# A fused attention and gated feed-forward kernel: the test of the limits moves from ahead of the banded path to behind it, and the planner gets a new table of ranks

## The chip, the cores and the metric

The kernel runs on one core of one Trainium2 chip. The metric is the device time of one execution in microseconds (us); lower is better. TensorE is called PE below (PEld is its weight load), VectorE DVE, ScalarE ACT, GpSimd POOL and SyncE SP.

## The reference

Attention with a few sink columns and a window, then a feed-forward layer. All inputs are float32 except the feed-forward weights, which are float64, and the two limits, which are 64-bit integers.

```
B, H, S, D = 4, 8, 768, 64          # n_sink = 4, window = 128
scores = q @ k.T / sqrt(D)
keep   = (col < n_sink) | ((0 <= row - col) & (row - col < window))
a      = softmax(where(keep, scores, -1e9))
x      = (a @ v) as (B*S, H*D) = (3072, 512)
h      = x @ w_in                   # (512, 2048)
g      = h * tanh(softplus(h))
y      = g @ w_out                  # (2048, 512)
```

## The kernel before

There are two paths in the program. `Fast` is the banded path: it is right when `n_sink <= 8`, `1 <= window <= 128`. `General` computes any limits. Both stand in the program as straight code without loops.

`body` starts with the prologue. SP issues the load of the limits (L978), then the keys, queries and values of the first two pairs of heads (L989 to L992). ACT loads its table (L981), writes two elements into each of three weight buffers (L985) and issues three loads of weights into them (L987, tiles `raw`). PE runs `WARM` = 24 products of zeros (L1000, "warm-ups") ahead of the first work. DVE builds constants, turns the limits into floats (L1004), makes a flag out of them in three small steps (L1009 to L1011) and then the three masks m0, m1, m2 (L961 to L968). Then each of the five engines reads the flag into a register (L1013), compares and branches (L1014): `Fast` follows straight on, `General` stands behind it and is jumped over at the end of `Fast`.

`Fast` cuts the work into 12 chunks of 256 rows, and in each chunk into four pairs of heads. For a pair, PE makes the scores (L442 for the first chunk of a batch, L445 for the others), DVE adds the mask and takes the row's minimum (L459), ACT the exponential (L462), DVE the reciprocal of the sum (L467, L468), DVE or ACT the normalisation (L476, L477), PE transposes (L487), ACT or DVE copies the result (L292, L294, L295) and PE multiplies by the values (L521). Next to that the weights, which come as float64, are taken apart into a high and a low part by ACT, DVE and POOL (L327 to L348, and the helpers L292, L295, L303, L305). The feed-forward layer runs per chunk in steps: L570 (first product), the activation in ACT and DVE (L580 to L587), L609 (second product). The last chunks end with L659 and L678, the scaling at L668 and the stores of y at L634 and L671.

The order of all this is not written by hand. Every operation is a task with a rank, the engines that may do it and a time; `Plan.solve` places the tasks one after the other, always the one that could start first, with `TILT` times its rank added. The ranks come from the tables `WI`, `WO` (weights) and `PAIRS` (pairs of heads), `EARLY` and `RING` hold when the loads of the prologue are expected, and `BANKS` says which PSUM buffers some tiles use. Where the plan leaves PE idle for more than `SPARE` = 250 ns, `emit` puts in products of zeros (L771, "fillers"), 75 of them in this kernel. Each engine then runs its tasks strictly in the plan's order.

## Time and profile before

| | |
|---|---|
| median of 3 runs | 690.08 us (689.73 to 690.75) |
| the profiled execution | 690.23 us, of which the profile's span is 688.4 us |
| PE busy | 679.2 us (99% of the span) |
| ACT busy | 525.4 us (76%) |
| DVE busy | 501.8 us (73%) |
| POOL busy | 124.4 us (18%) |

Shares are means over a front in which PE waits for the others and a long rest in which it does not, so they are to be read by stretch. The 1.8 us between the span and the execution's own time lie outside of what the profiler shows. A "PE busy" counts fillers and warm-ups too.

### The profile page before, as it was taken

Reading aid. Unit: us, or ns where it says so; the run is one execution under the profiler, and the core shown is the slowest. Engines: PE = TensorE matmul, PEld = TensorE weight load, DVE = VectorE, ACT = ScalarE, POOL = GpSimd, SP = SyncE. Lnnn points to the kernel's source line nnn. Section 1 sums busy time; section 2 is a strip of 40 time slices with the busy share of each in tenths; the row PEclk is TensorE's granted clock in tenths of the full one; section 3 lists DMA queues with packets and bytes.
Section 4 is the critical chain, followed back from the end, with each engine's and each line's share of the span. In section 5 each row is a group of like instructions: output and inputs, shape, how many; then the busy total and the mean of one; then the engine's idle time right before and its main releaser. Section 6 shows DMA issues by size and latency. Waiting matters only on the chain.

```text
span 688.4 us, 12130 instructions
## 1 busy us (share of the span) xinstructions
PE 679.2 (99%) x3980; PEld 563.6 (82%) x3980; DVE 501.8 (73%) x1442; ACT 525.4 (76%) x1223; POOL 124.4 (18%) x128
## 2 busy tenths in 40 slices
PE   8999999999999999999999999999999999999997
PEld 6778888988888888887888888887888787888885
DVE  8999999999896887666875886667677567432342
ACT  6999898987977876767876886778777676666672
POOL 1422321121104233120132131222010110000000
PEclk9999999999999999999999999999999999999999
DMA  6564343343535334041323331133340300010001
GB/s 211 175 185 124 123 139 114 116 135 98 161 97 156 88 83 134 16 110 39 95 79 91 112 86 55 40 86 95 101 109 1 86 0 25 1 62 0 1 0 67
DMA packets 49272, 60.20 MB, mean 87 GB/s; under 512 B 4912, under 2 KB 42160, under 8 KB 49200
## 3 DMA queue, kind: packets, MB, share of 16 engines
q1 hardware_dynamic: 48624, 57.69, 29.2%
q10 hardware_dynamic: 576, 1.64, 0.6%
q8 instruction: 34, 0.56, 0.3%
q14 instruction: 38, 0.31, 0.1%
HBM read 53.02 MB, written 6.29 MB: 86 GB/s over the span
## 4 chain that ended last, share of the span: by engine, by line
PE 84%; ACT 9%; DVE 5%; DMA 1%; issue 1%; ACTq 0%
PE hp L570 31%; PE acc L609 22%; PE att L609 12%; PE att L521 5%; PE att L445 5%; PE att L570 3%; ACT p L462 3%; PE att L487 2%; ACT p L477 1%; PE att L525 1%; ACT w L292 1%; ACT pth L292 1%; DMA raw<-w_in 1%; DVE u L587 1%; PE busy L1000 1%; ACT u L582 1%
## 5 line engine op out<-in xcount | busy, mean ns | idle before, releaser
L570 PE MATMUL hp<-w,w 128*128 128x256 f32 (+1 forms) x1440 | 269.8, 335 | 0.0
L570 PEld LDWEIGHTS hp<-w,w 128*128 128x128 f32 x1440 | 220.2, 189 | 28.3 <-issue 1.0
L609 PE MATMUL acc<-w,gh 128*128 128x512 f32 x500 | 137.9, 400 | 0.8 <-ACT w L292 0.5
L609 PEld LDWEIGHTS acc<-w,gh 128*128 128x128 f32 x500 | 87.7, 188 | 19.3 <-ACT gh L292 1.6
L462 ACT ACTIVATE p<-p,nm 128x136 f32<-128x136 f32 (+2 forms) x192 | 80.4, 428 | 21.2 <-DVE nm L459 20.6
L582 ACT ACTIVATE u<-u,bias 128x512 f32<-128x512 f32 x96 | 69.5, 724 | 35.0 <-DVE u L581 34.8
L587 DVE SCALAR_TENSOR_TENSOR u<-u,hp 128x512 f32<-128x512 f32 x88 | 60.1, 683 | 40.4 <-ACT u L586 37.8
L292 ACT ACTIVATE gh<-u 128x512 fp32r<-128x512 f32 x88 | 55.8, 634 | 33.7 <-DVE u L587 31.5
L580 ACT ACTIVATE u<-hp 128x512 f32<-128x512 f32 x88 | 52.5, 596 | 33.6 <-PE hp L570 32.0
L609 PE MATMUL acc<-w,gl 128*128 128x512 f32 x250 | 75.5, 394 | 0.0
L305 DVE TENSOR_TENSOR gl<-u,gh 128x512 fp32r<-128x512 f32 x72 | 51.8, 720 | 29.8 <-PE att L609 14.5
L584 ACT ACTIVATE u<-u,bias 128x512 f32<-128x512 f32 x96 | 69.6, 725 | 2.1
L303 POOL TENSOR_TENSOR w<-raw,w 64x400 fp32r<-64x400 f32 (+1 forms) x40 | 45.6, 1145 | 135.4 <-ACT w L292 50.9
L581 DVE TENSOR_SCALAR u<-u 128x512 f32<-128x512 f32 x96 | 43.0, 448 | 34.1 <-ACT u L580 33.7
L609 PE MATMUL att<-w,gh 128*128 128x512 f32 x244 | 67.5, 394 | 0.0
L586 ACT ACTIVATE u<-u 128x512 f32<-128x512 f32 x96 | 60.7, 632 | 1.9
L459 DVE CUSTOM_DVE_ANT_0 p<-att,m 128x136 f32<-128x136 f32 (+2 forms) x192 | 54.9, 313 | 3.1 <-PE att L442 1.2
L609 PEld LDWEIGHTS acc<-w,gl 128*128 128x128 f32 x250 | 46.2, 188 | 9.1 <-DVE gl L305 0.2
L457 DVE COPY_PREDICATED att<-behind,att 128x128 f32<-128x128 int32 x128 | 34.4, 292 | 25.6 <-PE att L445 25.0
L609 PEld LDWEIGHTS att<-w,gh 128*128 128x128 f32 x244 | 44.6, 188 | 8.8
L445 PEld LDWEIGHTS att<-w,w 128*128 128x128 f32 x256 | 41.1, 188 | 7.4 <-PE att L609 0.4
L445 PE MATMUL att<-w,w 128*128 128x264 f32 x256 | 45.8, 287 | 0.0
(115 smaller groups left out, 958.3 us busy)
## 6 DMA issues: line engine op xcount, KB each, us to landing
raw<-k_p SPq DMA_DIRECT2D x64, 200.0 KB, 3.4
raw<-q_p SPq DMA_DIRECT2D x64, 128.0 KB, 3.1
raw<-w_out SPq DMA_DIRECT2D x15, 512.0 KB, 3.6
raw<-w_in SPq DMA_DIRECT2D x14, 512.0 KB, 3.5
vt<-v_b SPq DMA_DIRECT2D x32, 192.0 KB, 2.6
y<-u SPq DMA_DIRECT2D x20, 256.0 KB, 2.1
ks<-k_p SPq DMA_DIRECT2D x16, 132.0 KB, 2.8
qh<-q_p SPq DMA_DIRECT2D x16, 128.0 KB, 2.9
```

Of the source, the lines that this page charges most:

```text
L292: ways[ACT] = act_t(n, psum), lambda: nc.scalar.activation(dst(), src(), AF.Copy, scale=scale or 1.0)
L305: way = dve_t(n), lambda: nc.vector.tensor_tensor(dst(), a(), b(), ALU.subtract)
L445: yield nc.tensor.matmul(st[e].t, part.t[:, e, cols], ks[e].t[:, c0:c0 + n], start=n_ == 0, stop=n_ == 1)
L459: a = add(r(.03 + .01 * e), {DVE: (dve_t(nw) + 8, lambda st=st, pv=pv, nm=nm, e=e, mask=mask, n=n, nw=nw: nc.vector.tensor_tensor_reduce(o ...
L462: a = add(r(.05 + .01 * e), {ACT: (act_t(nw, ptr=2), lambda pv=pv, nm=nm, i=i, e=e: nc.scalar.activation(pv(), pv(), AF.Exp, bias=nm.t[:, ...
L570: yield nc.tensor.matmul(out, w_.t[:, fs], x_, start=kt == 0 and n_ == 0, stop=kt == KT - 1 and n_ == 2)
L580: a = add(r + .5, {ACT: (act_t(N, True), lambda: nc.scalar.activation(u.t, hp.t, AF.Exp))}, g1, [hp], [u])
L582: sq = add(r + .52, {ACT: (act_t(N, ptr=1), lambda: nc.scalar.activation(u.t, u.t, AF.Square, bias=self.one)), DVE: shared((dve_t(N), lamb ...
L584: a = add(r + .53, {ACT: (act_t(N, ptr=1), lambda: nc.scalar.activation(u.t, u.t, AF.Ln, bias=self.half if sq.eng == ACT else self.one, sc ...
L586: a = add(r + .54, {ACT: (act_t(N), lambda: nc.scalar.activation(u.t, u.t, AF.Exp, scale=-1.0))}, [a], [u])
L587: e = add(r + .55, {DVE: (dve_t(N), lambda: nc.vector.scalar_tensor_tensor(u.t, u.t, 1.0, hp.t, ALU.subtract, ALU.mult))}, [a], [u, hp])
L609: yield nc.tensor.matmul(acc[at].t, g_.t[:, y, ts_], w_.t, start=new and n_ == 0, stop=done)
```

## The change

The flag and the branch go from ahead of `Fast` to behind it. `Fast` follows the prologue without a branch. Its last DVE operation is followed by the three steps that make the flag, then every engine reads it, compares, and jumps over `General` when the banded path was right (`General` would write y once more). The load of the limits moves from SP's queue to ACT's, ahead of ACT's table load. The part of the masks that only later chunks need (m2) becomes a task of the plan (`far`). `WARM` goes from 24 to 16. The planner gets new numbers (ranks, `EARLY`, `RING`, `BANKS`, two penalties), start times for ACT and DVE (`START`), and counts PE's tasks double for the first 1.5 us (`COLD`).

```diff
-WI = -8.52, -5.11, -2.45, -0.51, 7.12, ...
+WI = -13.89, -6.84, 0.25, -0.85, 5.69, ...
-PAIRS = (-17.41, -16.23, -9.53, ...
+PAIRS = (-15.84, -15.34, -4.82, ...
-WARM, SPARE, ROOM = 24, 250, 7
+WARM, SPARE, ROOM = 16, 250, 9
+START, COLD, FAR = {ACT: 550, DVE: 600}, 1500, 2
...
-        free = {e: 0.0 for e in (PE, ACT, DVE, POOL, SP)}
+        free = {e: START.get(e, 0.0) for e in (PE, ACT, DVE, POOL, SP)}
...
-            dur = t.ways[e][0]
+            dur = t.ways[e][0] * (2 if e == PE and at < COLD else 1)
...
+        self.plan.add(FAR, {DVE: shared((300, lambda: c.far()))})
...
+    def far():
         drop(c.m2[:, SK:], near, window)
-        behind(nc.vector.tensor_copy(c.m2[:, 0:SK], col[:, 0:SK]))
+        nc.vector.tensor_copy(c.m2[:, 0:SK], col[:, 0:SK])
...
-        nc.sync.dma_start(raw, limits.bitcast(I32).partition_broadcast(P))
+        nc.scalar.dma_start(raw, limits.bitcast(I32).partition_broadcast(P))
...
-            ok = tmp.tile([P, 1], F32, name="ok")
...
-            ready = nc.vector.scalar_tensor_tensor(flag, window_f, float(P), ok, ALU.is_le, ALU.mult)
-            c.masks(lambda x: tc.add_manual_dep(x.ins, ready.ins.name, nosync, reason="plan"))
-        banded = nc.values_load(flag[0:1, 0:1], min_val=0, max_val=1)
-        with tc.If(banded > 0) as cmp:
-            with ExitStack() as c2:
-                Fast(c2, tc, q, k, v, vs, w_in, w_out, out, c).run()
-        with cmp.Else():
+            c.masks()
+        with ExitStack() as c2:
+            Fast(c2, tc, q, k, v, vs, w_in, w_out, out, c).run()
+        ok, flag = top.tile([P, 1], F32, name="ok"), top.tile([P, 1], I32, name="flag")
+        nsink_f, window_f = lim[:, 0:1], lim[:, 1:2]
+        last = c.last[nc.vector.engine]
+        for ins in (nc.vector.tensor_scalar(ok, nsink_f, float(SK), None, ALU.is_le),
+                    nc.vector.scalar_tensor_tensor(ok, window_f, 1.0, ok, ALU.is_ge, ALU.mult),
+                    nc.vector.scalar_tensor_tensor(flag, window_f, float(P), ok, ALU.is_le, ALU.mult)):
+            tc.add_manual_dep(ins.ins, last.name, nosync, reason="plan")
+            last = ins.ins
+        banded = nc.values_load(flag[0:1, 0:1], min_val=0, max_val=1)
+        with tc.If(banded < 1):
             with ExitStack() as c2:
                 General(c2, tc, q, k, v, vs, w_in, w_out, out, c).run()
```

From the diff's first function on, line numbers of the changed kernel are 1 to 7 higher (L442 is L444 there, L459 L461, L668 L670).

The first place is the start of ACT's program, from its table load to its first normalisations. `raw_66` to `raw_68` are the three weight buffers, `p_...` the scores of a pair of heads (the first two pairs follow each other), `nm` their row minima. Before:

```order
L981 ACT_TABLE_LOAD
...
L987 DMA raw_68<-w_in 128x1024
L1013 TENSOR_LOAD flag
L1014 COMPARE_AND_BRANCH
L462 ACTIVATE p_11_0_196,sm_1_197<-p_11_0_196,nm_2_198 128x128 x2
L462 ACTIVATE p_11_0_196,sm_1_197<-p_11_0_196,nm_0_213 128x256 x2
L462 ACTIVATE p_22_0_217,sm_1_218<-p_22_0_217,nm_2_219 128x128 x2
L327 ACTIVATE w_0_237<-raw_67 128x512
```

And now:

```order
L984 DMA lim_raw<-limits 128x4
L987 ACT_TABLE_LOAD
...
L993 DMA raw_68<-w_in 128x1024
L464 ACTIVATE p_11_0_164,sm_1_165<-p_11_0_164,nm_2_166 128x128 x2
L329 ACTIVATE w_0_186<-raw_66 128x512
L464 ACTIVATE p_17_0_182,sm_1_183<-p_17_0_182,nm_2_184 128x128 x2
L464 ACTIVATE p_11_0_164,sm_1_165<-p_11_0_164,nm_0_194 128x256 x2
```

The flag's read and branch are gone from here, the limits' load stands first, and ACT's third operation of the path is now a step on the first weight buffer, `raw_66`, which DVE did before (L328).

The second place is PE's program from its last warm-up on; `att_...` are scores, `ks_60`, `qh_62` the first pair's keys and queries, `ks_61`, `qh_63` the second's. Before:

```order
L1000 MATMUL busy<-zero 128x224
L1013 TENSOR_LOAD flag
L1014 COMPARE_AND_BRANCH
L442 MATMUL att_0_188<-ks_60,qh_62 128x128
L442 MATMUL att_1_189<-ks_60,qh_62 128x128
L442 MATMUL att_0_192<-ks_60,qh_62 128x256
L442 MATMUL att_1_193<-ks_60,qh_62 128x256
...
L442 MATMUL att_0_206<-ks_61,qh_63 128x128
```

And now:

```order
L1005 MATMUL busy<-zero 128x224
L444 MATMUL att_0_158<-ks_60,qh_62 128x128
L444 MATMUL att_1_159<-ks_60,qh_62 128x128
...
L444 MATMUL att_0_170<-ks_61,qh_63 128x128
L444 MATMUL att_1_171<-ks_61,qh_63 128x128
L444 MATMUL att_0_178<-ks_60,qh_62 128x256
L444 MATMUL att_1_179<-ks_60,qh_62 128x256
```

The second pair's narrow scores now stand ahead of the first pair's wide ones. Over the whole path PE's program holds 75 fillers before and 69 now. Up to PE's first run of over fifty operations without a filler it is 60 before and 67 now; behind that run 15 before (4, and 11 ahead of one group of transposes) and 2 now.

The third place is the end of the path: DVE's last operations and what SP does behind its last store (`y`). On DVE before, and then now:

```order
L668 SCALAR_TENSOR_TENSOR w_0_7932<-att_0_7919,w_0_7873 128x128
L668 SCALAR_TENSOR_TENSOR w_0_7934<-att_0_7919,w_0_7873 128x128
L1014 UNCONDITIONAL_BRANCH
```

```order
L670 SCALAR_TENSOR_TENSOR w_0_7900<-att_0_7885,w_0_7834 128x128
L1018 TENSOR_SCALAR ok<-lim 128x1
L1019 SCALAR_TENSOR_TENSOR ok<-lim,ok 128x1
L1020 SCALAR_TENSOR_TENSOR flag<-lim,ok 128x1
L1023 TENSOR_LOAD flag
L1024 COMPARE_AND_BRANCH
```

On SP, now:

```order
L673 DMA y<-w_0_7898 128x128
L1023 TENSOR_LOAD flag
L1023 ISA x2
L1024 COMPARE_AND_BRANCH
```

Before, SP's last store was followed by the unconditional branch alone; now the read of the flag, two register steps and the comparison stand between them.

## Rows read from the trace of the kernel before

**Rows 1.** Busy time by stretch: length, then each engine's busy us (instructions), PEclk, DMA
```profile
10.00:60.00 50.00, 48.30 (x378) 36.77 (x379) 47.78 (x181) 49.96 (x160) 16.80 (x13) 1.00 0.59 172
...
100.00:150.00 50.00, 49.42 (x313) 43.44 (x313) 48.75 (x101) 45.59 (x92) 9.81 (x8) 1.00 0.41 128
...
200.00:683.00 483.00, 482.76 (x2643) 398.41 (x2642) 315.63 (x921) 346.76 (x785) 78.22 (x85) 1.00 0.23 64
```

**Rows 2.** The chain of waits in the first 60 us, start us, us, what
```profile
7.11 1.93 ACT p L462 x8
...
41.78 1.22 PE att L771 x11
```

**Rows 3.** Timeline of the first 14 us: start us, us, engine, line, operation [idle before]
```profile
0.73 1.28 ACT L981 ACT_TABLE_LOAD   x1 [0.73 <-PEq L1024]
0.74 0.39 SPq L978 DMA_DIRECT2D lim_raw<-limits  x1
...
2.26 0.38 ACTq L987 DMA_DIRECT2D raw<-w_in  x1
...
2.60 0.44 SPq L990 DMA_DIRECT2D qh<-q_p  x1
...
3.46 0.16 DVE L1004 SCALAR_TENSOR_TENSOR lim<-lim_raw 128x2 f32<-128x2 int32 x1 [0.28 <-DMA lim_raw<-limits]
...
3.65 0.15 DVE L1009 TENSOR_SCALAR ok<-lim 128x1 f32<-128x1 f32 x1
...
4.11 0.28 DVE L961 TENSOR_SCALAR col<-col,lim 128x128 f32<-128x128 f32 x1
...
5.30 0.16 DVE L968 COPY m<-col 128x8 f32<-128x8 f32 x1
...
5.80 1.53 PE L442 MATMUL att<-ks,qh 64*128 64x128 f32 x8
6.71 0.29 DVE L459 CUSTOM_DVE_ANT_0 p<-att,m 128x128 f32<-128x128 f32 x1 [1.25 <-PE att L442]
...
7.11 0.40 ACT L462 ACTIVATE p<-p,nm 128x128 f32<-128x128 f32 x1 [4.69 <-DVE nm L459]
...
7.14 0.42 DVE L328 TENSOR_SCALAR w<-raw 128x512 f32<-128x512 f32 x1
...
11.38 2.18 PE L771 MATMUL acc<-zero 128*128 128x224 bf16 x21
```

**Rows 4.** The warm-ups by line: duration ns min/median/max, first and last start us
```profile
L1000 PE MATMUL busy<-zero x24: 366/394/394, 1.0 to 5.3; 128*128 128x224 bf16 x24
```

**Rows 5.** The page's DMA issues: count, KB each, median us to landing
```profile
qh<-q_p SPq DMA_DIRECT2D x16, 128.0 KB, 2.9
```

**Rows 6.** Loads of the weight buffers that start in the first 30 us, issue to landing
```profile
DMA to landing us min/median/max: 3.4/4.2/6.3
```

**Rows 7.** The last operations of the path, timeline from 676 us
```profile
683.38 0.49 DVE L668 SCALAR_TENSOR_TENSOR w<-att,w 128x128 f32<-128x128 f32 x2 [0.58 <-PE att L659]
683.91 0.37 ACTq L671 DMA_DIRECT2D y<-w  x1
```

**Rows 8.** Flag read, branch and closing block by line: ns min/median/max, first and last start
```profile
L1013 SPq TENSOR_LOAD <-flag x1: 468/468/468, 4.2 to 4.2; - x1
...
L1014 ACTq COMPARE_BRANCH  x2: 38/38/39, 5.0 to 684.3; - x2
L1014 SPq COMPARE_BRANCH  x2: 46/48/49, 5.1 to 684.3; - x2
...
L1053 SPq EVENT_SEMAPHORE  x18: 17/17/28, 5.2 to 688.4; - x18
...
L1053 ACTq DRAIN  x2: 8/38/67, 687.0 to 687.9; - x2
```

**Rows 9.** DVE groups by shape: busy us, mean ns of one, idle before
```profile
L476 DVE TENSOR_SCALAR p<-p,rc 128x136 f32<-128x136 f32 x67 | 16.7, 290 | 0.6
...
L305 DVE TENSOR_TENSOR vss<-qh,vss 64x128 fp32r<-64x128 f32 x14 | 3.7, 288 | 0.4 <-ACT vss L292 0.2
```

## The prediction

> **What bounds the kernel now.** I read busy time by stretch first. From 200 us to 683 us PE is busy for 482.76 of 483.00 us, so there nothing but PE's own work counts, and the change takes none of that away. From 10 to 60 us it is the other way: ACT is busy for 49.96 of 50.00 us and DVE for 47.78, while PE's 48.30 are partly fillers [rows 1]. The reader is to see two regimes: a front in which ACT is the bound and PE waits, and a rest in which PE is. In the second one an earlier start is kept and nothing more is won. Then the chain of waits: up to 60 us it runs mostly through ACT's exponentials, and at 41.78 us through 11 fillers, 1.22 us, which is PE waiting for a group of transposes [rows 2]. Last the two ends. In front the first row minimum on DVE starts at 6.71 us after 1.25 us of idle time, and ACT's first exponential at 7.11 us, after 4.69 us of waiting [rows 3]. At the end the path's last DVE operations run from 683.38 to 683.87 us, the last store is issued at 683.91 us, ACT and SP branch at 684.3 us, and the closing block ends at 688.4 us [rows 7, 8].

> **The front: an earlier start.** The three steps of the flag lie between 3.65 us, where the first starts, and 4.11 us, where the first mask does: 0.46 us. Without them the last mask, which starts at 5.30 us and takes 0.16, ends at 5.00 us. PE's warm-ups follow each other in (5.3 - 1.0) / 23 = 0.187 us [rows 4]; 16 of them end at about 4.0 us, where 24 kept PE until the first scores at 5.80 us. The first queries are loaded on SP's queue, which loses the limits' load of 0.39 us from its front, and their load takes 2.9 us [rows 5]; they are there at about 4.1 us. So the scores are done before the masks are, DVE can take the first minimum at 5.00 us instead of 6.71, and ACT the first exponential at 5.40 us instead of 7.11 [rows 3]: **1.71 us earlier**. The limits themselves are as early as before: they were first on SP's queue at 0.74 us and are first on ACT's now, and DVE waited 0.28 us for them.

> **What is late next.** ACT's queue now has the limits' load of 0.39 us ahead of the table load (1.28 us, which started at 0.73) and of all that follows, so the first weights are issued at 2.26 + 0.39 = 2.65 us. On SP that load held back the first queries; on ACT it holds back the weights. The new order puts a step on those weights third on ACT, behind two exponentials of 0.40 us, at 6.20 us. A weight load takes 4.2 us in the median, 3.4 at least [rows 6], and DVE read this buffer at 7.14 us without waiting, so it took at most 7.14 - 2.26 = 4.88 us. That gives a wait on ACT of 2.65 + 4.2 - 6.20 = **0.65 us**, between nothing and 1.33. What is queued behind it is the second pair's exponentials, and the chain of the front goes through them. I take the median: of the lead 1.71 - 0.65 = **1.06 us** is left (0.38 to 1.71). The second pair's narrow scores also move ahead of the first pair's wide ones on PE; its queries were issued at 2.60 us and by 2.9 us of loading are there at some 5.2 us, before ACT is free, so I give that no price.

> **The new order.** What it does to PE's waiting I price by the fillers, which stand where the plan leaves PE without work: 13 fewer behind the first long run, 7 more ahead of it. One takes 2.18 / 21 = 0.104 us [rows 3]. That is 1.35 us less waiting at one place and 0.73 more at the other, net **0.62 us** less. The bounds are 1.35 us won, if the 7 only stand in place of warm-ups, and 0.73 lost, if the wait of the 11 comes back elsewhere because ACT has no time to spare. I take the net, since it counts both. m2's two steps, now a task of the plan, still stand on DVE ahead of the first minimum, so they are in the 5.00 us above. Penalties, `BANKS` and the ranks past 100 us I cost at nothing: PE's own backlog covers them (482.76 of 483.00 us), and if that cover fails it is the second rival below.

> **The end: a later branch.** The flag's steps took from 3.65 us to the read's start at 4.2 us, 0.55 us. Behind an end of 683.87 us the flag is there at 684.4 us. SP began the read at 4.2 us and branched at 5.1 us: 0.9 us for the read (0.468), the two register steps and the comparison [rows 8]. So SP branches at 685.3 us instead of 684.3: **1.0 us** later. From a branch over `General` to the next row ACT needs 687.0 - 684.3 = 2.7 us; that jump was there before and stays, and the stores land behind it. Nothing else waits for the branch, but nothing hides it either: the closing block begins with it. The lower bound is 0.6 us (flag and read alone); the upper is 2.3 us, if five engines that jump at the same time need half of 2.7 us more. The closing waits on SP are 17 to 28 ns each and may come twice, eight of them, 0.2 us, inside that bound.

> [...] The rows say 0.9 us from read to branch [rows 8]. [...]

> **The sum.** Of the profiled execution: 690.23 - 1.06 - 0.62 + 1.0 = 689.55 us. That execution lies 0.15 us above the median of the runs, 690.08, so against the median it is **689.4 us**, a gain of 0.68 us or 0.1%. A measurement of this kernel can tell 0.2%, that is 1.38 us, from no change; this one lies inside.

> **The rivals.**

> *The front is worth all of it.* The first weights land in time, the whole 1.71 us reach PE, and the wait at 41.78 us is gone without return. For it: those 11 fillers are one piece of the chain [rows 2]. Against it: ACT's 49.96 of 50.00 us, which leave no room to do the same work sooner. 690.08 - 1.71 - 1.35 + 1.0 = 688.0 us.

> *DVE becomes the bound between 100 and 150 us.* By a count of both programs, DVE takes 13 more normalisations from ACT (88 before) and 12 more of the small subtractions from POOL (14 before). At 0.290 and 0.288 us [rows 9] these are 7.2 us more. Between 100 and 150 us DVE is busy for 48.75 of 50.00 us and PE idles for 0.58 [rows 1]; what falls there beyond 1.25 us PE has to wait for. It decides against the change from 0.68 + 1.38 = 2.06 us of such waiting, that is with 3.3 of the 7.2 us in this stretch; with 4.8 of them it is 690.08 - 0.68 + 3.55 = 692.95, some 693.0 us. Against it: DVE has 483.00 - 315.63 = 167.37 us of idle time behind 200 us, and most of the path's pairs lie outside the stretch.

> *PE stays slow in front.* The warm-ups go at 0.187 us for 224 columns, the pace of 1.2 GHz; the filler at 11.38 us takes 0.104, that of 2.4 GHz (granted clock 1.00 from 10 us on) [rows 1, 3, 4]. With 16 warm-ups, 3 fillers and a wait for the second pair's queries PE does less before the first transposes. If it stays at the lower pace over eight more scores like those at 5.80 us (1.53 us), up to 1.53 us of chain are added; I take 1.0, since ACT works on meanwhile. 690.08 - 0.68 + 1.0 = 690.4 us. [...]

> **How the numbers follow.** The forecast 0.47, the full front 0.27, the slow PE 0.15, the DVE bound 0.11. Faster by over 0.2% is the second case, slower the fourth, and the first and third are both within 0.2%: 0.27, 0.62, 0.11. The known bounds reach from 690.08 - 1.71 - 1.35 + 0.6 = 687.6 us to the fourth case. I leave 2 in 10 out, the outermost part of the full front and the DVE case, and give **687.9 to 690.9 us**.

> **What would show it.** Right: DVE's first minimum near 5.0 us and ACT's first exponential near 5.4; a gap on ACT behind two exponentials that the load of the first weights ends; no chain of 11 fillers near 40 us; reads of the flag behind 684 us less the lead, and from the last L670 to the end of the span 1.0 us more than the 5.0 us between 683.38 and 688.4. Wrong: a first exponential later than 6 us (queries or limits late), an end longer by more than 1.6 us, or waits of PE for DVE's rows between 100 and 150 us. What would upset the number most is the new order's work between 10 and 60 us, where I price only fillers and not what ACT has to do before PE's backlog is formed.

## The result, and the profile after

| | before | after |
|---|---|---|
| median of the runs | 690.28 us (689.73 to 690.75, 4 runs) | 699.25 us (698.14 to 700.24, 4 runs) |
| ratio | | 1.0130 (95% interval 1.0110 to 1.0149) |
| the profiled execution, its span | 690.23 us, 688.4 | 700.24 us, 698.4 |
| TensorE's last matmul of the path starts | 683.1 us | 687.8 us |
| from its end to the span's end | 5.1 us | 10.3 us |

The change made the kernel 1.3% slower. The forecast was 689.4 us with a range of 687.9 to 690.9. Of the 10.0 us between the two profiled executions 4.8 are there before TensorE (PE) ends its last matmul, and 5.2 come behind it. The profiled execution of the changed kernel is the slowest of its four runs, 1.0 us above their median.

**The front.** The first group is of the timeline of the first 13 us of the changed kernel (start us, us, engine, line, operation, idle time before and what ended it); it answers to [rows 3].

```profile
0.74 0.41 ACTq L984 DMA_DIRECT2D lim_raw<-limits  x1
...
2.71 0.34 ACTq L993 DMA_DIRECT2D raw<-w_in  x1
...
3.88 0.16 DVE L1009 SCALAR_TENSOR_TENSOR lim<-lim_raw 128x2 f32<-128x2 int32 x1 [0.70 <-DMA lim_raw<-limits]
...
5.26 1.78 PE L444 MATMUL att<-ks,qh 64*128 64x128 f32 x12
5.34 0.29 DVE L461 CUSTOM_DVE_ANT_0 p<-att,m 128x128 f32<-128x128 f32 x1
...
5.74 0.40 ACT L464 ACTIVATE p<-p,nm 128x128 f32<-128x128 f32 x1 [2.87 <-DVE nm L461]
...
6.98 1.80 PE L773 MATMUL acc<-zero 128*128 128x224 bf16 x17
...
8.06 0.68 ACT L329 ACTIVATE w<-raw 128x512 f32<-128x512 f32 x1 [1.45 <-DMA raw<-w_in]
...
8.78 0.43 DVE L332 TENSOR_SCALAR w<-w 128x512 int32<-128x512 int32 x1 [1.57 <-ACT w L329]
...
12.42 1.51 PE L489 MATMUL att<-ident,p 128*128 128x128 f32 x6 [3.64 <-ACT p L479]
```

The start is earlier as forecast: the first exponential at 5.74 us instead of 7.11. But two exponentials later ACT stands for 1.45 us until the first weights land: issued at 2.71 us, they are there at 8.06, 5.35 us later. The second pair's exponentials are queued behind that step, DVE waits for it too, and PE, whose 17 fillers end at 8.78 us, stands for 3.64 us. Its first transposes start at 12.42 us; in the kernel before, at 10.57 (PE's row of its timeline):

```profile
10.57 0.96 PE L487 MATMUL att<-ident,p 128*128 128x128 f32 x6 [0.70 <-DVE p L476]
```

What that does to PE's clock is in the busy times by stretch of the changed kernel (length, then PE, PE's weight loads, DVE, ACT and POOL busy, granted clock, DMA share, GB/s; the last two answer to [rows 1]).

```profile
5.00:10.00 5.00, 3.78 (x32) 2.88 (x30) 3.30 (x21) 2.82 (x12) 0.00 (x0) 1.00 1.00 350
10.00:15.00 5.00, 2.58 (x13) 2.37 (x14) 4.58 (x15) 4.83 (x14) 0.00 (x0) 0.65 0.63 191
15.00:20.00 5.00, 5.00 (x27) 3.29 (x27) 3.64 (x15) 4.30 (x14) 0.00 (x0) 0.50 0.06 23
20.00:25.00 5.00, 5.00 (x42) 4.09 (x39) 3.74 (x15) 3.78 (x13) 1.28 (x1) 0.83 0.57 157
100.00:150.00 50.00, 50.00 (x325) 45.31 (x324) 49.01 (x99) 43.29 (x77) 9.11 (x7) 1.00 0.41 126
200.00:688.00 488.00, 487.00 (x2666) 401.50 (x2664) 319.14 (x948) 353.60 (x805) 64.92 (x67) 1.00 0.23 64
```

The granted clock is 1.00 between 5 and 10 us and then 0.65, 0.50 and 0.83: (0.35 + 0.50 + 0.17) x 5 / 0.5 = 10.2 us at the lower level (0.50), from 11.5 us, where PE still stands, to 21.7 us. Between 15 and 20 us PE is busy all the time and ACT, with 4.30 of 5.00 us, is not: the two have changed places. Between 100 and 150 us PE is busy for 50.00 of 50.00 us, so the waits for DVE that one rival put there did not come. From 200 us on PE idles for 1.00 us, where it had idled for 0.24.

**The end.** These rows of the changed kernel give flag read, branch and closing block by line (ns min/median/max, first and last start); they answer to [rows 7, 8]. SP's closing block of the kernel before follows them.

```profile
L661 PE MATMUL att<-w,w x18: 277/283/283, 685.8 to 687.8; 128*128 128x256 f32 x18
...
L1023 SPq TENSOR_LOAD <-flag x1: 517/517/517, 689.1 to 689.1; - x1
...
L1024 SPq COMPARE_BRANCH  x1: 50/50/50, 690.0 to 690.0; - x1
L1024 SPq EVENT_SEMAPHORE  x8: 17/17/17, 693.8 to 694.3; - x8
...
L1060 SPq EVENT_SEMAPHORE  x2: 28/28/28, 694.4 to 694.5; - x2
...
L1060 SPq EVENT_SEMAPHORE  x8: 17/28/28, 697.1 to 698.3; - x8
```

```profile
L1053 SPq EVENT_SEMAPHORE  x10: 17/28/28, 687.1 to 688.4; - x10
```

SP branches 1.9 us behind PE's last matmul (0.9 before), its next instruction comes 3.8 us later (2.8 before), eight waits, which the kernel before has in its front (from 5.2 us on), take 0.6 us here, and two waits into the closing block SP stands for 2.6 us (the hole, below). 1.0 + 1.0 + 0.6 + 2.6 = 5.2 us. The stores are not what it stands for: the last has landed by 690.3 us. The transfers in two windows of the same trace, 690.3 to 692 us and 694 to 696 us (queue, kind, packets, MB, share), are those of instructions, on q14 in pieces of 8 KB (over the whole run 40 with 0.33 MB):

```profile
q14 instruction: 4, 0.03, 6.4%
q8 instruction: 1, 0.02, 4.4%
...
q14 instruction: 4, 0.03, 5.3%
q8 instruction: 1, 0.02, 4.5%
```

One batch starts 0.6 us behind SP's branch, at 690.6 us, another at 694.1 us, 0.4 us after SP has gone on; between 692.1 and 694.1 us there is none. That SP stands until such a batch can be used is my reading of these times; e5 tests it for the hole.

### The profile page after: what moved, and what is told of

Same layout as the page of the kernel before. It is cut to its first block, busy times and chain, and to the rows that moved or that the text cites. A ratio compares the mean times of both kernels' runs of the same rounds, so it can differ in the third digit from the quotient of the medians.

```text
span 698.4 us, 12093 instructions
## 1 busy us (share of the span) xinstructions
PE 680.4 (97%) x3966; PEld 564.1 (81%) x3966; DVE 507.2 (73%) x1463; ACT 528.4 (76%) x1221; POOL 109.2 (16%) x109
## 4 chain that ended last, share of the span: by engine, by line
PE 68%; ACT 2%; DVE 1%; POOL 0%; issue 0%; ACTq 0%; POOLq 0%
PE hp L572 25%; PE acc L611 15%; PE att L611 12%; PE att L447 4%; PE att L523 4%; PE att L572 3%; PE att L489 2%; PE att L527 1%; PE acc L680 1%; PE att L506 1%; ACT p L464 0%; PE att L661 0%; PE att L680 0%; DVE w L307 0%; ACT w L294 0%
## 5 line engine op out<-in xcount | busy, mean ns | idle before, releaser
L611 PE MATMUL acc<-w,gh 128*128 128x512 f32 x500 | 135.2, 396 | 0.0
L305 POOL TENSOR_TENSOR w<-raw,w 64x400 fp32r<-64x400 f32 (+1 forms) x34 | 38.0, 1122 | 174.9 <-ACT w L294 82.1
L461 DVE CUSTOM_DVE_ANT_0 p<-att,m 128x136 f32<-128x136 f32 (+2 forms) x192 | 55.1, 314 | 4.2 <-PE att L444 2.5
L305 POOL TENSOR_TENSOR gl<-u,gh 128x512 fp32r<-128x512 f32 x19 | 24.6, 1293 | 175.4 <-PE att L611 104.9
L459 DVE COPY_PREDICATED att<-behind,att 128x128 f32<-128x128 int32 x128 | 34.2, 292 | 18.8 <-PE att L447 18.2
```

Source lines behind the costliest of these rows:

```text
L305: ways[POOL] = pool_t(n), lambda: nc.gpsimd.tensor_tensor(dst(), a(), b(), ALU.subtract)
L461: a = add(r(.03 + .01 * e), {DVE: (dve_t(nw) + 8, lambda st=st, pv=pv, nm=nm, e=e, mask=mask, n=n, nw=nw: nc.vector.tensor_tensor_reduce(o ...
L611: yield nc.tensor.matmul(acc[at].t, g_.t[:, y, ts_], w_.t, start=new and n_ == 0, stop=done)
```

## The experiments

**Theory A**, stated ahead of the first runs: two costs with nothing to do with each other, the branch behind the path (5.2 us) and the late first weights with the clock that falls behind PE's stall (4.8 us). The rivals are named in the expectations. Medians below are of 4 runs unless said otherwise; the kernel before, timed beside them, had medians of 689.7 to 690.3 us.

**Parts of the change undone (e1 to e4).** e1 puts the test ahead again, e2 takes the tables, limits' queue and warm-ups of before, e3 is the changed kernel with one line back, e4 has no test:

```diff
-        nc.scalar.dma_start(raw, limits.bitcast(I32).partition_broadcast(P))
+        nc.sync.dma_start(raw, limits.bitcast(I32).partition_broadcast(P))
```

> The changed kernel's tables, order and limits' queue, with the test put back ahead of the banded path. Theory A (two separate costs: 5.2 us at the end from the branch behind the path, 4.8 us in front because the first weights come later than the order counts on, so that TensorE stands still and its clock falls to half for 10 us): the end's 5.2 us go, the front's stay, since the weights land when they did, near 8.0 us: 695 us (694 to 696), half clock still in the records from about 11.5 us. Rival B (the earlier start itself makes the front slow, because loads that now start before 7 us get in the way of the first weights): with the test ahead the loads start late again and both costs go: 690 to 691 us. Rival C (the new order is no worse and all of the loss is the branch): 689 to 690 us.

Measured: 694.58 us, ratio 1.0057 (1.0041 to 1.0074). Within theory A's range by the sum, but not by the parts: 7.1 us follow PE's last matmul, because here too SP stands in the closing block (1.8 us), and the front loses 2.2 us and not 4.8. PE's first scores start at 5.66 us instead of 4.26, the transposes at 12.53, PE stands for 2.54 us, and the granted clock is 1.00 in every stretch up to 680 us. Rival B's reason does not hold: the weights are taken at 8.17 us here and at 8.06 in the changed kernel, late in both. What goes with the earlier start is a stall that is 1.1 us longer, and the fall of the clock with it.

> The tables, limits' queue and 24 warm-ups of the kernel before, with the test behind the path. Theory A: the end costs its 5.2 us; in front the order of before meets an earlier start, wins up to 1 us if its first weights hold no one up and loses some if they do: 694 to 697 us, at full clock from about 7 us on. Rival B (the earlier start makes the front slow): 698 to 700 us, with half clock in the front. Rival C (the branch is all of the loss): 699 to 700 us.

Measured: 694.48 us, 1.0055 (1.0034 to 1.0075), with a granted clock of 1.00 in every stretch up to 680 us and 10.7 us behind PE's last matmul. The test's move alone costs 4.3 us in the tables of before. PE's last matmul starts at 681.6 us, 1.5 sooner than before, but that is hardly the move: PE's work is 0.3 us ahead up to 100 us, and the rest comes between 100 and 132 us, where PE is busy for 32.00 of 32.00 us here and in e8 and for 31.42 in the kernel before, which waits there for 0.5 us until ACT has done a step on a late weight.

> The changed kernel with the limits' load issued first on SP's queue again; nothing else changes. Theory A: the first weights' load is issued 0.4 us sooner and lands some 0.4 us sooner, the stall of TensorE shortens by as much, the clock still falls: 698.0 to 699.3 us, 0 to 1 us less than the changed kernel. Rival D (the limits' load ahead of the weights on ScalarE's queue is what makes them late): weights land near 6.5 us as before and most of the front's 4.8 us goes: 695 to 696 us.

Measured: 697.15 us, 1.0098 (1.0079 to 1.0116): 2.1 us less than the changed kernel, between theory A and rival D. ACT takes the weights 1.8 us sooner and without waiting:

```profile
6.27 0.65 ACT L329 ACTIVATE w<-raw 128x512 f32<-128x512 f32 x1
```

The wait that is left is PE's for the second pair's queries, 1.43 us up to 6.78 us, and the clock falls behind it too, for 3.4 us.

```diff
...
-        banded = nc.values_load(flag[0:1, 0:1], min_val=0, max_val=1)
-        with tc.If(banded < 1):
-            with ExitStack() as c2:
-                General(c2, tc, q, k, v, vs, w_in, w_out, out, c).run()
```

> The changed kernel without the three flag steps, the read, the branch and the general path: limits that ask for the general path are not served. It measures what the end costs in all. Theory A: the front is untouched and the end is that of a program with no branch: 5 us or more less than the changed kernel, 693 to 694.5 us. Recorded forecast (the later branch costs 1.0 us): 698 us. If the jump of 2.7 us that the kernel before has in its front falls on nothing either way, the end after TensorE's last matmul is about 5 us, as before.

Measured: 691.45 us (10 runs), 1.0018 (1.0007 to 1.0029), 1.6 us below theory A's range. Behind PE's last matmul are 3.4 us: at the end a branch behind the path costs 6.9 us, one ahead of it, with its jump over `General`, 1.7 (2.0 in e8, 2.4 in e7). PE's work ends 2.0 us sooner than in the changed kernel's profile. With it goes the clock, which is at half for 3.4 us only, though PE stalls nearly as long (3.32 us, transposes at 12.47); that the clock is the reason is inferred here and tested in e6.

**The hole in the closing waits (e5).** Dead instructions in SP's program, in the path that is not run:

```diff
         with tc.If(banded < 1):
+            for _ in range(14):
+                nc.sync.dma_start(raw, limits.bitcast(I32).partition_broadcast(P))
```

> The changed kernel with 14 more loads of the limits on SP's queue inside the general path, which is not run here: dead instructions that only push the closing block of SP's program further along. Theory A (the end pays for fetching instructions twice: once at the jump's target, and once more 10 instructions behind it, because a fetched piece of SP's program happens to end there): the jump's 3.7 us stay, the second hole of 2.7 us in SP's closing waits goes or moves: 696.5 us (696 to 697.2), and SP's closing waits then stand without a hole. Rival E (the hole is a wait for a semaphore of another engine or of a store): it stays between the same two waits, 699.3 us.

Measured: 695.70 us, 1.0081 (1.0056 to 1.0105); from PE's last matmul to the end 7.5 us, 2.7 less. SP's closing block of this kernel, by line as above:

```profile
L1024 SPq EVENT_SEMAPHORE  x8: 17/17/17, 692.5 to 693.0; - x8
...
L1062 SPq EVENT_SEMAPHORE  x10: 17/28/28, 693.1 to 694.3; - x10
```

Eighteen waits follow each other without a hole. Nothing that is executed was changed, so the hole is a matter of where the instructions lie, and rival E falls. That a piece of 8 KB ends there is theory A's reading, which the run fits. The other runs agree: of those with the branch behind the path, the four with dead loads (e5, e12, f4, g1) have no hole and the nine without have one of 1.3 to 3.2 us. (Of the 3.55 us that the median fell, 0.8 are not the hole; the profile shows half clock for 6.8 us where the changed kernel's had 10.2.)

**The clock (e6).** 30 more fillers in the changed kernel's first long run of them (`more` starts at 30):

```diff
-                    for _ in range(int((t.start - at - SPARE) / (n / (1.2 if at < SLOW else 2.4) + 2.5) + 1)):
+                    m = int((t.start - at - SPARE) / (n / (1.2 if at < SLOW else 2.4) + 2.5) + 1)
+                    if m > 9 and more:
+                        m, more = m + more, 0
+                    for _ in range(m):
```

> The changed kernel with 30 more filler matmuls on TensorE in its idle stretch ahead of the first transposes, about 3.1 us at the pace of 0.104 us; the weights land as late as before. Theory A (part of the front's loss is the clock that falls after TensorE has stood still): no half clock behind 11 us, the first transposes still near 12.4 us, 1.5 to 2.5 us less than the changed kernel: 697.3 us (696.7 to 698). Rival F (the stretch at half clock costs nothing, because ScalarE and VectorE set the pace there): 699.3 us, however the clock stands.

Measured: 697.19 us, 1.0102 (1.0076 to 1.0127), 2.06 us less than the changed kernel; the two sets of four runs overlap by 0.2 us. All of it lies ahead of the end: PE's last matmul starts 2.1 us sooner, and 10.4 us follow it. Busy times by stretch and the timeline's row of the first transposes:

```profile
10.00:15.00 5.00, 4.73 (x45) 4.13 (x44) 4.56 (x17) 5.00 (x17) 0.00 (x0) 1.00 0.54 185
15.00:20.00 5.00, 5.00 (x46) 3.62 (x45) 5.00 (x20) 5.00 (x17) 0.73 (x1) 1.00 0.32 92
```

```profile
12.64 0.97 PE L489 MATMUL att<-ident,p 128*128 128x128 f32 x6 [0.27 <-ACT p L479]
```

The transposes start no sooner, but the clock stays at 1.00 and six of them take 0.97 us instead of 1.51. Work that computes nothing made the kernel 2 us faster; rival F falls.

**The limits' load (e7, e9, f1).** e7 is the kernel before with that one load on ScalarE's queue.

> The kernel before with the limits' load on ScalarE's queue and nothing else changed. Theory A (the small packets of that load stand ahead of the first weights' and make them land 1.8 us later, near 8 us; what this costs hangs on where the order wants the weights): the order of before puts its first weight step on ScalarE at 9.7 us, so that the late landing is covered: 690 to 690.8 us. Rival D (the load's place costs 2 us in any order): 692 us.

Measured: 691.94 us (10 runs), 1.0027 (1.0013 to 1.0042). My expectation missed, and rival D's 692 us came: the load's place costs 1.8 us in the order of before and 2.1 in the new one (e3). The order of before isn't covered, because its first weight step stands on DVE, ahead of the minima of the first pair's wide scores. DVE's row in the timeline:

```profile
8.75 0.43 DVE L328 TENSOR_SCALAR w<-raw 128x512 f32<-128x512 f32 x1 [1.98 <-DMA raw<-w_in]
```

Before, the same row stands at 7.14 us with no wait [rows 3]. Then, whether it is the value loads that now run beside the weights:

```diff
+        twin = top.tile([P, 4], I32, name="lim_twin")
+        nc.sync.dma_start(twin, limits.bitcast(I32).partition_broadcast(P))
```

> The changed kernel with a second load of the limits, into a tile that nothing reads, first on SP's queue; the limits that are used still load on ScalarE's queue. Theory H (the limits' load of 128 tiny packets was a brake on SP's queue: without it the key, query and value loads run ahead, and the value loads' 512-byte packets run beside the first weights' from 3.5 us on and stretch their landing): with the brake back the first weights land near 6.5 us, though the limits stay ahead of them on ScalarE's queue, and the time falls as it did with the limits back on SP's queue: 697.2 us (696.3 to 698). Rival I (the tiny packets hold up the weights on their own queue): the weights land near 8 us and the time stays at 699.3 us.

Measured: 698.56 us, 1.0117 (1.0094 to 1.0140), and no answer: with a load of the limits on either queue both queues were late, the limits came at 5.5 us (3.9 in the changed kernel), PE's first scores at 6.36 and the weights at 8.57.

```diff
-            nc.sync.dma_start(held["vt"][pr][:, :, 0:2, :], ...)
+            nc.scalar.dma_start(held["vt"][pr][:, :, 0:2, :], ...)
```

> The changed kernel with the two value loads issued on ScalarE's queue behind the three weight loads, in place of SP's; the limits stay first on ScalarE's queue. Theory H (the value loads, which begin at 3.5 us once the limits no longer go ahead of them on SP's queue, run beside the first weights' packets and stretch their landing): the first weights land near 6.5 to 7 us and 1 to 2 us of the time go: 697.2 to 698.2 us. Rival I (the limits' packets ahead of the weights on their own queue are the cause): landing near 8 us, 699.3 us.

Measured: 697.29 us, 1.0111 (1.0094 to 1.0128). The weights are taken at 7.5 us, between the two theories:

```profile
L329 ACT ACTIVATE w<-raw x1: 671/671/671, 7.5 to 7.5; 128x512 f32<-128x512 f32 x1
```

So the value loads are a part of it, 0.5 us of the 1.8. The time fell by more than these 0.5 us can explain: in this profile the clock does not fall in front at all, and the four runs spread from 696.3 us (mean granted clock 0.994) to 698.6 (0.990). What is shown is that the load which shares a queue with the limits' is the one that comes late. With the limits on SP's queue it is the second pair's queries: in g1 below PE waits for them until 7.13 us, in the changed kernel PE takes them at 5.26 us without waiting. The 128 packets of 4 KB of the first weights run from 4.3 to 8.1 us in the changed kernel and from 4.1 to 6.1 in the one before; why they are spread out so stays open.

**The warm-ups (e8).** In the kernel before:

```diff
-WARM, SPARE, ROOM = 24, 250, 7
+WARM, SPARE, ROOM = 16, 250, 7
```

> The kernel before with 16 warm-ups in place of 24 and nothing else changed. Theory A (in the kernel before it is the warm-ups, not the test, that hold TensorE's first scores back, by half a microsecond to one): the first scores start 0.5 us sooner and the first exponential too; the order runs 0.3 to 0.8 us sooner from there if the clock holds: 689.5 us. Rival G (fewer warm-ups cost TensorE its clock in the front): half clock in the records before 20 us and 691 us or more.

Measured: 689.44 us (10 runs), 0.9994 (0.9984 to 1.0004). PE's first scores start at 5.17 us instead of 5.80 and its last matmul at 681.8, and from 9.5 us on it runs at the faster pace (8 fillers in 0.94 us); the gain is not larger than what can be told.

**The new order (e10, e11, g2).** e10 has the ranks, penalties and banks of before with the new start and landing times, e11 the reverse; both have the test behind and the limits on SP's queue; e10 has 16 warm-ups, e11 24. g2 is the new order alone, test and limits as before.

The core of e10's edit, from e3; e11 puts the plus lines of the change into e2 (the other tables likewise):

```diff
-PEN_C, PEN_S, PEN_N, PEN_J, PEN_Q = 50.59, 0, 7.89, 0, 3443.15
+PEN_C, PEN_S, PEN_N, PEN_J, PEN_Q = 50.59, 0, 2.67, 0, 3392.52
-WI = -13.89, -6.84, 0.25, -0.85, 5.69, ...
+WI = -8.52, -5.11, -2.45, -0.51, 7.12, ...
```

> Test behind the path, limits on SP's queue, 16 warm-ups and the changed planner's start and landing times, with the ranks, penalties and banks of the kernel before. Between the run with the tables of before (694.5 us) and the one with all the new tables (697.2 us), 2.7 us apart. Theory J (the new ranks cost it, most of it where TensorE waits for VectorE near 222 us): 693.5 to 695 us. Rival K (the start and landing times cost it, since they set the front): 696.5 to 697.5 us.

> The counterpart: test behind, limits on SP's queue, 24 warm-ups and the start and landing times of before, with the new ranks, penalties and banks. Theory J (ranks): 696.5 to 697.5 us, with TensorE waiting for VectorE between 200 and 240 us. Rival K (times): 694 to 695 us.

Measured: 697.72 us, 1.0108 (1.0084 to 1.0132), and 699.37 us, 1.0126 (1.0102 to 1.0150). Both theories miss: with none of the two the median is 694.5 us, with both 697.2, and each half alone costs as much as both or more. Ranks and times work together, so the order's cost cannot be split that way. The end is no reason: by the start of PE's last matmul the four are at 681.6, 684.2, 684.2 and 687.1 us (none, both, times, ranks).

> The changed kernel's tables, planner and 16 warm-ups with the test ahead of the path and the limits on SP's queue, both as before: the new order alone. Theory A (the order itself loses 1 to 2.5 us: its wait for VectorE near 222 us, and 0.5 us elsewhere): 692 us (691 to 693), of which up to 1.8 us can be a hole in the closing waits. Rival C (the new order is no worse, it was only held up by the late weights): 689.5 to 690.5 us with no hole.

Measured: 694.18 us, 1.0061 (1.0042 to 1.0080), more than expected: 6.9 us behind PE's last matmul, with a hole of 1.9 us in the closing waits, and a last matmul at 685.0 us, 3.2 later than in e8, which has the same test, queue and warm-ups. A part of that is the wait near 222 us. In e3, which has the same order:

```profile
220.00:225.00 5.00, 4.25 (x31) 3.61 (x31) 4.97 (x14) 3.76 (x10) 2.99 (x3) 1.00 0.45 116
```

And in the kernel before:

```profile
220.00:225.00 5.00, 5.00 (x38) 4.77 (x37) 3.22 (x13) 3.58 (x10) 1.48 (x2) 1.00 0.36 105
```

DVE is busy for 4.97 of 5.00 us and PE idles for 0.75, for a group of transposes that DVE's step on a weight holds back. In the kernel before DVE has 3.22 us to do in the same stretch and PE 5.00. From 60 to 682 us PE idles for 2.0 us in g2 and for 0.6 in e8, and near 46 us it stands for another 1.0 us until ACT has copied a transpose; the rest of the 3.2 us was not traced. The changed kernel has that second wait too (PE's row of its timeline):

```profile
46.03 0.48 PE L444 MATMUL att<-ks,qh 64*128 64x128 f32 x2 [0.96 <-ACT pth L294]
```

**Can the move pay (e12, f2, f3)?** e12 is e2 with 16 warm-ups and the dead loads; f2 has the changed kernel's flag and read ahead and the branch alone behind; f3 is the kernel before with `General` first in the program, so that the jump is taken ahead:

```diff
-        with tc.If(banded > 0) as cmp:
+        with tc.If(banded < 1) as cmp:
+            with ExitStack() as c2:
+                General(c2, tc, q, k, v, vs, w_in, w_out, out, c).run()
+        with cmp.Else():
             with ExitStack() as c2:
                 Fast(c2, tc, q, k, v, vs, w_in, w_out, out, c).run()
-        with cmp.Else():
-            with ExitStack() as c2:
-                General(c2, tc, q, k, v, vs, w_in, w_out, out, c).run()
```

> The tables and limits' queue of the kernel before, test behind, 16 warm-ups, and 14 dead loads in the general path that move SP's closing block off the end of a fetched piece. Theory A (the branch behind the path costs 2.2 us more at the end than the one ahead even without the second hole, and wins 0.7 us in front): 690.5 us (690 to 691.5), no better than the kernel before and about 1 us above the one with the test ahead and 16 warm-ups. Rival C, refined (without the hole and the late weights the move pays): under 689.4 us.

Measured: 691.66 us (10 runs), 1.0025 (1.0013 to 1.0037), just above theory A's range; some 1 us of it lies outside the profile's span (2.1 to 3.2 us in these runs, 1.8 to 1.9 in the kernel before), which no run explains. It doesn't pay: 7.5 us behind PE's last matmul, and that matmul starts at 682.0 us, not sooner than in e8 (681.8), though the first scores start 0.83 us sooner. The next late things take the lead: PE stands for 1.55 us until DVE has done its step on the first weights, and the records show half clock for 3.4 us from 7.5 us on.

```diff
...
+        banded = nc.values_load(flag[0:1, 0:1], min_val=0, max_val=1)
         with ExitStack() as c2:
             Fast(c2, tc, q, k, v, vs, w_in, w_out, out, c).run()
...
-        banded = nc.values_load(flag[0:1, 0:1], min_val=0, max_val=1)
         with tc.If(banded < 1):
```

> The changed kernel with the three flag steps and the read of the flag back ahead of the path and the branch alone behind it. Theory A: of the 10.25 us behind TensorE's last matmul the flag, read and register steps (1.5 us) go, the jump, the repeated waits and the hole in the closing waits (if it falls on them again) stay: 8.7 us; in front the read holds the engines back by 0.5 to 1 us, which the late weights hide: 697.8 us (697 to 699). Recorded step (the flag and the read are nearly all of the later branch's price): the tail returns to 5.1 to 6.1 us and the time to 695 us.

Measured: 694.57 us, 1.0063 (1.0046 to 1.0080), 3.2 us less than expected. The end is 7.7 us: flag and read are worth 1.2 us there, the jump is still 3.7, and the hole is 1.3 here. The rest is the front: the first scores start at 5.49 us, PE stalls for less (2.73 us), and the clock stays up, as in e1 (mean granted clock over the span 0.996 and 0.998, 0.987 in the changed kernel).

> The kernel before with the two paths' places exchanged: the general path stands first in the program and is jumped over ahead of the banded path, and no jump stands behind it. Theory L (a jump costs about the same 2.7 to 3.7 us wherever nothing hides it; ahead of the path the loads hide a part): the end shortens by 1.7 us to 3.4 us, the first exponential comes 1.5 to 2.5 us later than 7.1 us: 690 to 691.5 us. Rival M (in front the loads of the weights hide the jump): 688.5 us.

Measured: 693.47 us, 1.0047 (1.0030 to 1.0064), above both theories. The end shortens to 3.6 us, as expected, but the front loses over 5 us. The branch on PE's queue, by line, and PE's next row in the timeline:

```profile
L1014 PEldq COMPARE_BRANCH  x1: 6444/6444/6444, 4.8 to 4.8; - x1
```

```profile
11.43 1.66 PE L442 MATMUL att<-ks,qh 64*128 64x128 f32 x8 [5.74 <-issue]
```

A jump that is taken while the DMA engines are full (share 1.05 up to 8.5 us) costs PE 6.4 us; the same branch, not taken, 0.09. The first instruction transfers come at 8.5 us, 3.7 us behind the branch, where they came after 0.6 us at the end of the changed kernel. Behind PE's standing still the clock is at half from 9.0 to 19.3 us, which is in the front's loss too. The kernel before has its branch ahead almost for nothing because it falls through.

**Do the costs add (f4, g1)?** f4 has limits on SP's queue, dead loads and 30 fillers; g1 is f4 without the fillers.

> The changed kernel with three repairs at once: limits on SP's queue, 30 fillers ahead of the first transposes, and the dead loads in the general path. Theory A (the costs add: 2.1 us for the queue, 2.7 us for the hole, and what is left of the clock): 693.9 us (693.2 to 694.8), the rest over the kernel before being the branch behind the path (2.2 to 2.4 us) and the new order (1.2 to 2 us). Rival N (the order that was tuned with the change takes back what the repairs give): 690.5 us or less.

Measured: 696.79 us, 1.0101 (1.0084 to 1.0117), 2.9 us more than expected. The fillers themselves were in the way: with the weights in time there was little stall to fill, PE was at the lower clock for 3.4 us, and the row reads

```profile
8.91 6.06 PE L776 MATMUL acc<-zero 128*128 128x224 bf16 x47
```

so that the transposes started at 14.81 us. The fillers that shortened one front lengthened the other.

> The changed kernel with the limits on SP's queue and the dead loads in the general path, without more fillers. Theory A (the two costs add): the run with the limits on SP's queue alone gave 697.15 us, its hole in the closing waits was 2.3 us: 694.8 us (694.3 to 695.4). Rival N (the order takes back what a repair gives): 696.5 us or more.

Measured: 694.79 us, 1.0071 (1.0052 to 1.0090), as theory A has it: the queue's 2.1 us and e3's hole of 2.3 us add. PE's rows of g1's first 14 us, and then those of g2, the same order with the test ahead:

```profile
4.37 0.80 PE L444 MATMUL att<-ks,qh 64*128 64x128 f32 x4 [0.17 <-DMA qh<-q_p]
...
7.13 2.58 PE L444 MATMUL att<-ks,qh 64*128 64x128 f32 x12 [1.29 <-DMA qh<-q_p]
9.65 3.36 PE L773 MATMUL acc<-zero 128*128 128x224 bf16 x17
12.80 0.97 PE L489 MATMUL att<-ident,p 128*128 128x128 f32 x6
```

```profile
5.33 0.80 PE L444 MATMUL att<-ks,qh 64*128 64x128 f32 x4 [1.13 <-SPq L1057]
...
6.89 2.58 PE L444 MATMUL att<-ks,qh 64*128 64x128 f32 x12
9.40 2.10 PE L773 MATMUL acc<-zero 128*128 128x224 bf16 x17
12.13 1.03 PE L489 MATMUL att<-ident,p 128*128 128x128 f32 x6 [0.63 <-ACT p L479]
```

The scores of g1 start 0.96 us sooner, its transposes 0.67 later, and the last matmul of both starts at 685.0 us. Two things eat the lead: the wait for the queries, and in this profile PE's pace, since g1's 17 fillers take 3.36 us, 0.198 each, near the 0.187 of the warm-ups, where those of g2 take 2.10, 0.124 each. The test ahead of the path delays nothing that isn't late anyway.

## Why the prediction was wrong

One way from the kernel before to the changed one, by medians: the new order alone 694.18 (+4.1, of which 1.8 is the longer end), with the test behind 697.15 (+3.0), with the limits on ScalarE's queue 699.25 (+2.1). All three parts cost; the forecast had all three together at -0.7.

- **The front: an earlier start**: nearly the right size (first minimum 5.34 us, first exponential 5.74, forecast 5.0 and 5.4). "The limits themselves are as early as before" was wrong: DVE has them at 3.88 us, not 3.46, which accounts for the 0.34 us. The step from the start to the sum failed. The lead of 1.06 us is worth nothing: g1 against g2 and e12 against e8 start 0.96 and 0.83 us sooner and end PE's work within 0.2 us of each other.
- **What is late next**: the right wait, mis-sized. I took the median landing of 4.2 us and bounded it by 4.88; it was 5.35 us, because what shares the limits' queue comes later by more than the 0.4 us of the issue. ACT's wait of 1.45 us (0.65 forecast) is above my bound of 1.33. I carried a landing over from a trace in which another load stood ahead of it.
- **PE stays slow in front** was the rival that came nearest, priced at 1.0 us and up to 1.53: the clock takes 2.06 us (e6), but not by the rival's mechanism. The two paces that it calls 1.2 and 2.4 GHz are columns per nanosecond in the traces: 224 columns in the 0.187 us of a warm-up, and, at the end of the path before, 256 columns in the 0.107 us by which one of 18 products of 512 columns (L678, 4.08 us) takes longer than one of 18 of 256 (L659, 2.16 us). I had thought of a clock that comes up late. That did not come here, 12 scores from 5.26 us on take 1.78 us (in g2 2.58); what came is a clock that is up, is lost behind a stall of 3.64 us and stays down for 10.2 (granted 0.50). In e6, where fillers leave 0.27 us of the stall, it stays at 1.00.
- **The new order**: forecast 0.62 us less by the fillers; it is 1.9 us more on PE against the kernel before and 3.2 against e8. Fillers say where a plan expects to wait, not where PE waits. The 11 near 40 us are gone, as forecast, and PE stands still for 0.96 us at 46 us instead.
- **The end: a later branch**: forecast 1.0 us, bounded by 2.3; it is 5.2. The flag and the read, which I priced at all of it, are 1.2 us (f2) and so nearly right. "That jump was there before and stays" failed: it is 1.0 us longer, the waits that come twice took 0.6 us instead of 0.2, and the hole of 2.6 us I did not have at all. That five engines jump at once is not shown to be the reason for the 1.0 us: at the end SP's jump takes 2.7 to 3.6 us in the five kernels that have the test ahead and `General` behind (3.6 in e7, which is the kernel before but for one queue) and 3.6 to 3.9 in the thirteen that have it behind. SP stands still twice, for 3.8 us behind its branch and for 2.6 us in the closing block, and a batch of instruction transfers starts within the first, at 690.6 us, and one 0.4 us ahead of the second, at 694.1. That it stands for them is my reading; e5 shows that the second hangs on where dead code lies.
- **DVE becomes the bound between 100 and 150 us**: not there (PE 50.00 of 50.00 us), but near 222 us, for 0.75 us. **The front worth all of it**: falls with the first point.

## What to carry to other kernels

A lead at the start is worth what the next late thing leaves of it: before counting it, list what the order wants first and when each load can be there in the new queue order, and take no landing time from a trace in which the queue was filled otherwise. A branch cost PE 0.09 us here where it was not taken, and the test ahead of the path cost nothing where PE waited anyway (g1 and g2 start PE's last matmul at 685.0 us); behind the last store each part of it is on the path. A taken jump cost SP 2.7 to 3.9 us there, and a second hole of up to 3.2 us came and went with the layout of the code, so look at the trace for holes between waits that are long fulfilled. When PE stands still in a front, look at the granted clock behind it: here 10.2 us at 0.50 followed a stall of 3.64 us, and filling the stall was worth 2.06 us (e6).
